# Two second-layer products at a time in chunks 3 to 6 of a memory-attention mixer

## The chip, the core and the metric

The kernel runs on one core of a Trainium2 chip. The time is the device time of one execution in microseconds (us). A run is repeated and the median taken; the kernel before took 741.93 us (three runs, 741.67 to 742.0). One execution was also recorded by the profiler, and the rows below come from it.

TensorE is written PE, its weight loads PEld, ScalarE is ACT, VectorE is DVE, GpSimd is POOL, SyncE (which issues most DMAs) is SP.

## The reference

Attention through 32 memory slots is followed by a mixer over tokens and one over channels:

```python
k_m = einsum('bhsm,bhsd->bhmd', softmax(phi), k)        # memory keys, v_m alike
attn = softmax(scale * q @ k_m.T) @ v_m                 # batch 8, heads 8, seq 576, head_dim 64
x = attn.transpose(0, 2, 1, 3).reshape(8, 576, 512)
h = relu(x.transpose(0, 2, 1) @ w_tok1) @ w_tok2        # 576 -> 256 -> 576
u = x + h.transpose(0, 2, 1)
out = u + relu(u @ w_ch1) @ w_ch2                       # 512 -> 1536 -> 512
```

All of it is float32. The kernel splits each operand into a high and a low part, and makes a product of three matmuls: high by high, high by low, low by high.

## The kernel before

The 8 x 576 rows are cut into nine chunks of 512 rows. Attention and the token mixer of a batch ("steps" of a quad of heads, functions whose names begin with step) are spread over the channel mixer of the chunks before it. Chunks 0 to 2 run the channel mixer plainly, chunks 7 and 8 together in another way at the end. The change touches chunks 3 to 6.

In these, the first layer (512 to 1536) is made in six pieces of 256 hidden features, numbered 0 to 5 here, by seven block products in the place of eight. The function `quarters` writes out one piece. The products are named by their operands, in the order "11", "21", "T2", "T1", "T3", "22", "T4". I call them A0, B1, A2, B3, A4, B5 and A6: the letter tells which PSUM tile takes the result (`qa` or `qb`), and the number the position. Each is six matmuls of 128x256 (line 335). A and B are the two buffers of one PSUM pool. A2 adds onto what A0 left in its bank, so it may start only when ACT has copied A0's result out (line 2167, `whole<-qa`). In the same way B3 follows the copy of B1, A4 that of A2, B5 that of B3 (`whole<-qb`), and A6 that of A4. The result of B5 is taken by DVE, that of A6 by ACT and DVE. A piece has five copies by line 2167, one each for A0 to A4. Each engine's instructions stand in its queue in the order in which the program writes them.

The second layer (1536 to 512) is accumulated in four banks, `acc0` to `acc3`, one for 128 output channels. For one hidden block of 128 features and one of the four channels it takes three matmuls of 128x512 (line 197). A piece brings two hidden blocks, so eight such groups of three stand in `todo`, and the next piece issues them between its products.

After each product comes `point(x)`, with x = 0, 0.5, ..., 3, and a last `point(3.5)` after `point(3)`. Each is a half slot. It first runs what the table `events` holds for it (`run`): loads, casts, a step of attention, the input preparation of a later chunk. Then `mix()` issues one group of three from `todo`. So a piece without steps reads on PE: A0, group, B1, group, A2, group, B3, group, A4, group, B5, group, A6, group, group.

Other work that the argument meets, all of it put between the products by `events`: the casts `a<-aT` (line 826, ACT) and their low halves (line 827, POOL) in `a_pair`; the casts `vv<-vh` (line 840, ACT) in `v_pairs`; the casts of the next chunk's operands `x<-u` and `xT<-t` (line 284, ACT); the exponential of the scores (line 776, ACT) after the subtraction of their maxima (line 771, DVE). `add` in `quarters` is line 2170 (DVE).

Of the kernel before, what the change touches and what calls it, by code (L numbers as in the profile page):

```python
# [27 lines left out]
def kernel(  # L28
# [30 lines left out]
    B, _, _, _, NC, _, D = kv.shape  # L59
# [78 lines left out]
    def relu_high(h, ps):  # L138
        nc.scalar.activation(out=h, in_=ps, func=AF.Relu)  # L139

    def relu_low(h, l, ps):
        nc.vector.scalar_tensor_tensor(  # L142
            out=l, in0=ps, scalar=0.0, in1=f32(h), op0=ALU.max, op1=ALU.subtract
        )
# [423 lines left out]
    def load_unit(n, eng=nc.scalar):  # L568
        m = n - 2 * NF * (DOUBLE - WIN + 1)
        if m >= 7 * NF // 4:  # L570
            return
        p, j = n // 4 % (NF // 2), n % 4
        t = sb.tile([P, 1024], F32R, tag="c1", name=f"unit{n}", bufs=NF)
        if m >= 0:
            units[n] = t.rearrange("p (o x m) -> p o x m", o=2, x=2)
            eng.dma_start(out=f32(t), in_=Sums2.to[:, m // (NF // 4), m % (NF // 4)])
            return
        units[n] = t.rearrange("p (o x a n) -> p o x a n", o=2, x=2, a=2)
        m = 512 if j == 3 else 1024
        nc.scalar.dma_start(out=f32(t)[:, :m], in_=sums[p].to[:, j, :m])  # L580
# [1416 lines left out]
    events = {}  # L1997
# [63 lines left out]
    for c in range(2, DOUBLE + 1):  # L2061
        h = 2 * NF * (c - 1)
# [18 lines left out]
    for c in range(DOUBLE):  # L2081
        h = 2 * NF * (c + 1)
# [15 lines left out]
    for p in range(NF // 2):  # L2098
        x, h = Sums2(p), 2 * NF * (WIN + min(p, 4)) + (8.5 if not p else (3.5, 1.5, 9.5)[max(p - 3, 0)])
# [8 lines left out]
    double, h = Double(DOUBLE), 2 * NF * DOUBLE  # L2108
# [14 lines left out]
    def run(h, *ks):  # L2123
        for k in ks:
            for fn, x in events.pop((h, k), ()):
                out = fn(*x)
                if callable(out):
                    out()
# [20 lines left out]
    def quarters(c, p):  # L2149
        ch, h, n = chunks[c], 2 * NF * c + 4 * p, 4 * ((c - WIN) * NF // 2 + p)  # L2150
        todo = [(x, f, a) for x, f in before if f < x.end for a in range(NKK)]
        before[:] = [(ch, 2 * p), (ch, 2 * p + 1)]
        (eh, el), (oh, ol) = ch.pieces(p)
        t0, t1 = slice(0, HW), slice(HW, CW)

        def mix(n=1):
            for x, f, a in todo[:n]:
                x.ch2(f, [a])
                if f == x.end - 1:
                    x.add(a)  # L2160
            del todo[:n]

        def tile(x):
            return pch.tile([P, CW], F32, tag="ch", name=f"{x}{p}" + ch.n, bufs=2)

        def out(to, ps):
            nc.scalar.copy(out=to, in_=ps[:, :HW])  # L2167

        def add(to, x, y):
            nc.vector.tensor_tensor(out=to, in0=x, in1=y, op=ALU.add)  # L2170

        def product(ps, k, name, first):
            if not k % 2:
                load_unit(n + k // 2 + AHEAD)
            ch.product(ps, units[n + k // 2][:, k % 2], name, first, name in ("21", "22", "T4"))

        if not whole:
            whole.append(sb.tile([P, 2, CW], F32, tag="c1", name="whole", bufs=NF))
        et, ot = whole[0][:, 0], whole[0][:, 1]

        def split_relu(h, l, x):
            relu_high(h, x)
            relu_low(h, l, x)

        def point(x):
            run(h + x, -1, 0, 1)
            mix()

        a = tile("qa")
        product(a, 0, "11", True)  # L2190
        out(et[:, t0], a)
        point(0)
        b = tile("qb")
        product(b, 1, "21", True)
        out(ot[:, t0], b)
        add(et[:, t0], et[:, t0], ot[:, t0])
        point(0.5)
        product(a, 2, "T2", False)
        out(et[:, t1], a)
        split_relu(eh[:, t0], el[:, t0], et[:, t0])  # L2200
        point(1)
        product(b, 3, "T1", True)
        out(ot[:, t0], b)
        point(1.5)
        product(a, 4, "T3", False)
        out(ot[:, t1], a)
        add(ot[:, t1], ot[:, t0], ot[:, t1])
        point(2)
        product(b, 5, "22", False)
        add(et[:, t1], b[:, :HW], et[:, t1])  # L2210
        split_relu(oh[:, t1], ol[:, t1], ot[:, t1])
        point(2.5)
        product(a, 6, "T4", False)
        split_relu(eh[:, t1], el[:, t1], et[:, t1])
        split_relu(oh[:, t0], ol[:, t0], a[:, :HW])
        point(3)
        point(3.5)

    for c in range(WIN, DOUBLE):
        for p in range(NF // 2):  # L2220
            quarters(c, p)
# [13 lines left out]
    for p in range(NF // 2):  # L2235
        h, n = 2 * NF * DOUBLE + 4 * p, n0 + 4 * p
# [63 lines left out]
    for i, name in enumerate(double.order[:-1]):  # L2300
        y = name in ("21", "T1", "22")
        for p in range(NF // 2):
            k = i * (NF // 2) + p
# [117 lines left out]
```

## Time and profile before

| | |
|---|---|
| median of three runs | 741.93 us (741.67 to 742.0) |
| the profiled execution | 741.64 us, of which the recorded span is 739.7 us |
| PE busy | 733.8 us, 99% of the span |
| PEld busy | 627.3 us, 85% |
| DVE, ACT, POOL busy | 494.2, 344.2, 72.1 us |
| products of chunks 3 to 6 (line 335) in the span | from 298.3 us to 614.7 us |

A row of the timeline gives the start in us from the beginning of the span, the duration, the engine, the line of the kernel, the operation, the output and inputs by name, partitions and elements, and a count if neighbouring instructions were merged. In brackets stands how long the engine sat idle before, and what released it. A matmul's duration covers its way through the array, so that neighbours overlap; the distance between starts is what a matmul costs. Weight loads run ahead of the matmul that uses them.

### The profile page before, as it was taken

Reading aid. Unit: us, or ns where it says so; the run is one execution under the profiler, and the core shown is the slowest. Engines: PE = TensorE matmul, PEld = TensorE weight load, DVE = VectorE, ACT = ScalarE, POOL = GpSimd, SP = SyncE. Lnnn points to the kernel's source line nnn. Section 1 sums busy time; section 2 is a strip of 40 time slices with the busy share of each in tenths; the row PEclk is TensorE's granted clock in tenths of the full one; section 3 lists DMA queues with packets and bytes.
Section 4 is the critical chain, followed back from the end, with each engine's and each line's share of the span. In section 5 each row is a group of like instructions: output and inputs, shape, how many; then the busy total and the mean of one; then the engine's idle time right before and its main releaser. Section 6 shows DMA issues by size and latency. Waiting matters only on the chain.

```text
span 739.7 us, 12859 instructions
## 1 busy us (share of the span) xinstructions
PE 733.8 (99%) x4889; PEld 627.3 (85%) x4889; DVE 494.2 (67%) x896; ACT 344.2 (47%) x742; POOL 72.1 (10%) x71
## 2 busy tenths in 40 slices
PE   9999999999999999999999999999999999999998
PEld 8678787787888888899898889888998998888887
DVE  4989873776567657766586738674676455655874
ACT  5789754242314243554463536363544462444431
POOL 1021014001022020110010101010101000000000
PEclk9999999999999999999999999999999999999999
DMA  9965530585825564869587858777667975776862
GB/s 358 415 230 178 218 106 1 136 260 145 260 90 169 168 201 107 285 189 310 163 270 252 252 214 228 259 212 278 167 203 246 305 218 174 256 256 208 272 217 86
DMA packets 98813, 158.33 MB, mean 214 GB/s; under 512 B 42208, under 2 KB 65632, under 8 KB 94304
## 3 DMA queue, kind: packets, MB, share of 16 engines
q1 hardware_dynamic: 80320, 98.92, 41.3%
q10 hardware_dynamic: 18432, 58.60, 25.0%
q8 instruction: 39, 0.64, 0.3%
q14 instruction: 22, 0.18, 0.1%
HBM read 121.57 MB, written 35.91 MB: 213 GB/s over the span
## 4 chain that ended last, share of the span: by engine, by line
PE 94%; DVE 3%; DMA 1%; ACT 1%; issue 0%; POOL 0%; POOLq 0%; DVEq 0%; ACTq 0%; SPq 0%
PE acc L197 29%; PE cp L174 12%; PE qa L335 9%; PE u L935 7%; PE qb L335 7%; PE e L455 7%; PE da L400 4%; PE db L400 3%; PE Ap L895 3%; PE Rp L914 1%; PE sp L754 1%; PE u L1617 1%; PE end L455 1%; PE sp L655 1%; PE u L1394 1%; PE pp L1269 1%
## 5 line engine op out<-in xcount | busy, mean ns | idle before, releaser
L197 PE MATMUL acc<-qhh,c 128*128 128x512 f32 x256 | 98.6, 395 | 0.0
L197 PE MATMUL acc<-hh,c 128*128 128x512 f32 x288 | 96.7, 395 | 0.0
L335 PEld LDWEIGHTS qb<-x,unit 128*128 128x128 f32 x432 | 60.9, 188 | 6.8 <-ACT whole L2167 0.7
L335 PEld LDWEIGHTS qa<-xT,unit 128*128 128x128 f32 x432 | 60.8, 188 | 6.8 <-ACT whole L2167 0.8
L197 PEld LDWEIGHTS acc<-hh,c 128*128 128x128 f32 x288 | 54.1, 188 | 14.5 <-issue 3.4
L335 PE MATMUL qa<-xT,unit 128*128 128x256 f32 x432 | 63.0, 281 | 0.0
L335 PE MATMUL qb<-x,unit 128*128 128x256 f32 x432 | 63.0, 281 | 0.0
L827 POOL TENSOR_TENSOR a<-aT,a 64x576 fp32r<-64x576 f32 x22 | 33.9, 1542 | 294.9 <-ACT a L826 294.1
L197 PE MATMUL acc<-hl,c 128*128 128x512 f32 x144 | 56.3, 391 | 0.0
L197 PEld LDWEIGHTS acc<-qhh,c 128*128 128x128 f32 x256 | 48.2, 188 | 9.5 <-issue 3.3
L197 PE MATMUL acc<-qal,c 128*128 128x512 f32 x192 | 53.7, 394 | 0.0
L142 DVE SCALAR_TENSOR_TENSOR hl<-cp,hh 128x512 fp32r<-128x512 f32 x36 | 24.7, 686 | 40.6 <-ACT hh L139 40.5
L174 PE MATMUL cp<-uh,c1h 128*128 128x512 f32 x144 | 51.3, 397 | 0.0
L197 PE MATMUL acc<-qhl,c 128*128 128x512 f32 x128 | 50.7, 396 | 0.0
L174 PE MATMUL cp<-ul,c1h 128*128 128x512 f32 x144 | 50.3, 390 | 0.0
L174 PE MATMUL cp<-uh,c1l 128*128 128x512 f32 x144 | 50.3, 390 | 0.0
L2170 DVE TENSOR_TENSOR whole<-whole 128x256 f32<-128x256 f32 x48 | 25.5, 531 | 37.0 <-ACT whole L2167 36.8
L2167 ACT COPY whole<-qa 128x256 f32<-128x256 f32 x72 | 26.8, 372 | 48.9 <-PE qa L335 47.0
L197 PEld LDWEIGHTS acc<-qal,c 128*128 128x128 f32 x192 | 32.7, 189 | 3.6
L142 DVE SCALAR_TENSOR_TENSOR qhl<-whole,qhh 128x256 fp32r<-128x256 f32 x48 | 22.1, 459 | 18.4 <-ACT qhh L139 18.1
L2167 ACT COPY whole<-qb 128x256 f32<-128x256 f32 x48 | 17.7, 369 | 34.9 <-PE qb L335 34.6
L174 PEld LDWEIGHTS cp<-uh,c1l 128*128 128x128 f32 x144 | 27.0, 188 | 5.7
(295 smaller groups left out, 1650.2 us busy)
## 6 DMA issues: line engine op xcount, KB each, us to landing
unit<-sums ACTq DMA_DIRECT2D x93, 512.0 KB, 4.3
kv<-in_kv_dram SPq DMA_DIRECT2D x12, 1280.0 KB, 8.8
rawc<-in_w_ch_dram SPq DMA_DIRECT2D x12, 1024.0 KB, 6.2
q<-in_q_dram SPq DMA_DIRECT2D x16, 576.0 KB, 6.2
unit<-sums SPq DMA_DIRECT2D x18, 512.0 KB, 4.8
unit<-sums ACTq DMA_DIRECT2D x30, 256.0 KB, 3.8
sums<-sums SPq DMA_DIRECT2D x12, 512.0 KB, 5.6
sums<-v SPq DMA_DIRECT2D x12, 512.0 KB, 6.9
```

What stands on the lines that cost most here:

```text
L142: nc.vector.scalar_tensor_tensor(out=l, in0=ps, scalar=0.0, in1=f32(h), op0=ALU.max, op1=ALU.subtract)
L174: nc.tensor.matmul(ps, l[:, a, w], r[:, a], start=n == 0, stop=n == len(mm) - 1)
L197: nc.tensor.matmul(ps, l_[f // 2][:, f % 2, a * P : (a + 1) * P], r[:, w], start=f == start and x == 0, stop=f == end - 1 and x == 2,)
L335: nc.tensor.matmul(ps[:, :HW], l, r, start=first and n == 0, stop=n == len(mm) - 1, skip_group_check=not first,)
L400: nc.tensor.matmul(ps, l, r, start=first and n == 0, stop=n == len(mm) - 1, skip_group_check=not first,)
L455: nc.tensor.matmul(ps, weights[:, x, m], r[:, w], start=first and n == 0, stop=last and n == 2, skip_group_check=name in ("T2", "T3", "22"),)
L655: nc.tensor.matmul(s.kvp[32 * i : 32 * i + 32, :KV], s.pt[:, i, j, :], s.kv[:, 4 * j + i], start=j == 0, stop=j == NC - 1,)
L827: s.low_eng.tensor_tensor(out=l, in0=s.aT[own], in1=f32(h), op=ALU.subtract)
L895: nc.tensor.matmul(ps[:, :TT], a, w, start=x == 0, stop=x == len(mm) - 1)
L935: nc.tensor.matmul(ps[:, :HALF], a, r, start=x == 0, stop=x == len(mm) - 1)
L2167: nc.scalar.copy(out=to, in_=ps[:, :HW])
L2170: nc.vector.tensor_tensor(out=to, in0=x, in1=y, op=ALU.add)
```

## The change

`point` no longer issues a group at every half slot. It counts the groups that are owed. If neither this half slot nor the next one holds a function whose name begins with `step`, the first owed group is held back and the two are issued together at the next point. Where a step is near, and at the end of a piece, everything owed is issued at once.

```diff
+        owed = [0]
...
         def point(x):
+            busy = any(k[0] in (h + x, h + x + 0.5) and fn.__name__.startswith("step")
+                       for k, v in events.items() for fn, _ in v)
             run(h + x, -1, 0, 1)
-            mix()
+            owed[0] += 1
+            if busy or owed[0] > 1 or x == 3.5:
+                mix(owed[0])
+                owed[0] = 0
```

The number of instructions is the same on every engine. ACT, POOL and SP issue theirs in the same order as before. On DVE one addition out of an `acc` bank in chunk 3 changes places with an `add` of the piece. PE's order changes in 17 of the 24 pieces; in the other seven (piece 3 of each chunk, and piece 0 of chunks 4 to 6) it is the same. A product into B now directly follows a product into A at 41 places more than before.

The first place is piece 5 of chunk 3, from A2 or B3 to B5. PE before, from B3 on; `qb` and `qa` are the PSUM tiles of the products, `acc` the banks of the second layer:

```order
L335 MATMUL qb_3_3901<-x_2649,unit_3809 128x256 x6
L197 MATMUL acc_3_3320<-qal_3_3705,c_1065 128x512
L197 MATMUL acc_3_3320<-qal_3_3706,c_1065 128x512
L197 MATMUL acc_3_3320<-qal_3_3705,c_1065 128x512
L335 MATMUL qa_3_3875<-xT_3_3028,unit_3844 128x256 x6
L197 MATMUL acc_3_3256<-qhh_3_3707,c_1065 128x512
L197 MATMUL acc_3_3256<-qhl_3_3708,c_1065 128x512
L197 MATMUL acc_3_3256<-qhh_3_3707,c_1065 128x512
L335 MATMUL qb_3_3901<-x_3_3080,unit_3844 128x256 x6
```

PE now at the same place, from A2 to B5:

```order
L335 MATMUL qa_3_3875<-xT_3_2986,unit_3806 128x256 x6
L335 MATMUL qb_3_3898<-x_2649,unit_3806 128x256 x6
L197 MATMUL acc_3_3299<-qal_3_3705,c_1065 128x512
L197 MATMUL acc_3_3299<-qal_3_3706,c_1065 128x512
L197 MATMUL acc_3_3299<-qal_3_3705,c_1065 128x512
L197 MATMUL acc_3_3320<-qal_3_3705,c_1065 128x512
L197 MATMUL acc_3_3320<-qal_3_3706,c_1065 128x512
L197 MATMUL acc_3_3320<-qal_3_3705,c_1065 128x512
L335 MATMUL qa_3_3875<-xT_3_3028,unit_3841 128x256 x6
L335 MATMUL qb_3_3898<-x_3_3076,unit_3841 128x256 x6
```

B3 has moved ahead of a group, to stand right behind A2; A4 has as many groups ahead of it as before; and the group between A4 and B5 has moved behind B5.

The second place is piece 1 of chunk 4, which begins with steps. PE before, from A2 to B5's neighbourhood:

```order
L335 MATMUL qa_4_4187<-xT_4_3949,unit_4110 128x256 x6
L197 MATMUL acc_4_4295<-qhh_4_4017,c_521 128x512
L197 MATMUL acc_4_4295<-qhl_4_4018,c_521 128x512
L197 MATMUL acc_4_4295<-qhh_4_4017,c_521 128x512
L335 MATMUL qb_4_4254<-x_3452,unit_4110 128x256 x6
L197 MATMUL acc_4_4307<-qhh_4_4017,c_521 128x512
L197 MATMUL acc_4_4307<-qhl_4_4018,c_521 128x512
L197 MATMUL acc_4_4307<-qhh_4_4017,c_521 128x512
L335 MATMUL qa_4_4187<-xT_4_3934,unit_4148 128x256 x6
```

PE now, from A2 on:

```order
L335 MATMUL qa_4_4187<-xT_4_3946,unit_4110 128x256 x6
L335 MATMUL qb_4_4254<-x_3452,unit_4110 128x256 x6
L197 MATMUL acc_4_4303<-qhh_4_4017,c_521 128x512
L197 MATMUL acc_4_4303<-qhl_4_4018,c_521 128x512
L197 MATMUL acc_4_4303<-qhh_4_4017,c_521 128x512
L197 MATMUL acc_4_4307<-qhh_4_4017,c_521 128x512
L197 MATMUL acc_4_4307<-qhl_4_4018,c_521 128x512
L197 MATMUL acc_4_4307<-qhh_4_4017,c_521 128x512
L335 MATMUL qa_4_4187<-xT_4_3934,unit_4148 128x256 x6
L335 MATMUL qb_4_4254<-x_4_4006,unit_4148 128x256 x6
```

The steps and the products up to A2 stand where they stood; from there on B3 and B5 each come one group earlier, and A4 where it was.

## Rows read from the trace of the kernel before

**Rows 1.** The page: its first line, and the shares of the chain of work that ended last, by engine.

```profile
span 739.7 us, 12859 instructions
...
PE 94%; DVE 3%; DMA 1%; ACT 1%; issue 0%; POOL 0%; POOLq 0%; DVEq 0%; ACTq 0%; SPq 0%
```

**Rows 2.** The waits of PEld between 300 and 628 us: who waited for whom, us in total, times, longest.

```profile
PEld qb L335 <- ACT whole L2167: 0.7, 2, 0.3
```

**Rows 3.** The timeline of PE in piece 5 of chunk 3: A0, a group, B1, the next group, and B5.

```profile
366.00 0.88 PE L335 MATMUL qa<-x,unit 128*128 128x256 f32 x6
366.72 0.86 PE L197 MATMUL acc<-qal,c 128*128 128x512 f32 x3
367.41 0.87 PE L335 MATMUL qb<-x,unit 128*128 128x256 f32 x6
368.12 0.86 PE L197 MATMUL acc<-qal,c 128*128 128x512 f32 x3
...
373.04 0.87 PE L335 MATMUL qb<-x,unit 128*128 128x256 f32 x6
```

**Rows 4.** The timeline of ACT, POOL and DVE in piece 5 of chunk 3: the copy of A0, a cast for POOL, POOL's two instructions, the first `add` of the piece on DVE, two casts of line 840, the copy of B3, and the second `add`.

```profile
366.97 0.37 ACT L2167 COPY whole<-qa 128x256 f32<-128x256 f32 x1 [1.53 <-PE qa L335]
...
367.24 0.67 ACT L826 CAST a<-aT 64x576 fp32r<-64x576 f32 x1
...
368.06 3.00 POOL L827 TENSOR_TENSOR a<-aT,a 64x576 fp32r<-64x576 f32 x2 [29.44 <-ACT a L826]
...
368.78 0.98 DVE L2170 TENSOR_TENSOR whole<-whole 128x256 f32<-128x256 f32 x1 [0.75 <-ACT whole L2167]
...
371.09 0.61 ACT L840 CAST vv<-vh 64x128 fp32r<-64x128 f32 x2 [0.49 <-POOL a L827]
...
372.25 0.37 ACT L2167 COPY whole<-qb 128x256 f32<-128x256 f32 x1
...
374.19 0.43 DVE L2170 TENSOR_TENSOR whole<-whole 128x256 f32<-128x256 f32 x1 [0.93 <-ACT whole L2167]
```

**Rows 5.** PE at 390 us, where two groups of the second layer stand side by side.

```profile
390.19 1.55 PE L197 MATMUL acc<-qal,c 128*128 128x512 f32 x6
391.57 0.64 PE L335 MATMUL qa<-x,unit 128*128 128x256 f32 x4
```

**Rows 6.** The timeline of PE in piece 0 of chunk 3: a product into A that directly follows one into B, and what follows it.

```profile
307.69 0.88 PE L335 MATMUL qa<-xT,unit 128*128 128x256 f32 x6
308.41 0.29 PE L935 MATMUL u<-a,vv 128*128 128x288 f32 x1
```

**Rows 7.** DVE and PE at the end of piece 1 and the beginning of piece 2 of chunk 4: the instruction that empties the bank of A6, and B1, which takes that bank next.

```profile
406.83 0.41 DVE L142 SCALAR_TENSOR_TENSOR qhl<-qa,qhh 128x256 fp32r<-128x256 f32 x1
...
407.71 0.87 PE L335 MATMUL qb<-x,unit 128*128 128x256 f32 x6
```

**Rows 8.** The copy of B3 and B5 in other pieces, two rows for each: piece 2 of chunk 3, piece 2 of chunk 5, piece 5 of chunk 5.

```profile
331.93 0.37 ACT L2167 COPY whole<-qb 128x256 f32<-128x256 f32 x1
332.72 0.87 PE L335 MATMUL qb<-x,unit 128*128 128x256 f32 x6
...
493.88 0.37 ACT L2167 COPY whole<-qb 128x256 f32<-128x256 f32 x1
494.29 0.98 PE L335 MATMUL qb<-x,unit 128*128 128x256 f32 x6
...
534.05 0.37 ACT L2167 COPY whole<-qb 128x256 f32<-128x256 f32 x1
534.85 0.40 PE L335 MATMUL qb<-x,unit 128*128 128x256 f32 x2
```

**Rows 9.** All engines in piece 2 of chunk 4: the copy of B3, the weight load of B5, B5 itself, the group behind it, and A0 of the next piece.

```profile
412.97 0.36 ACT L2167 COPY whole<-qb 128x256 f32<-128x256 f32 x1
...
413.38 0.76 PEld L335 LDWEIGHTS qb<-x,unit 128*128 128x128 f32 x6 [0.32 <-ACT whole L2167]
413.39 0.97 PE L335 MATMUL qb<-x,unit 128*128 128x256 f32 x6
...
414.19 0.40 PE L197 MATMUL acc<-qhh,c 128*128 128x512 f32 x1
...
417.14 0.64 PE L335 MATMUL qa<-x,unit 128*128 128x256 f32 x4
```

**Rows 10.** All engines in piece 1 of chunk 4: the copy of A2, the exponential, the copy of B3, and B5.

```profile
399.49 0.37 ACT L2167 COPY whole<-qa 128x256 f32<-128x256 f32 x1 [1.00 <-PE qa L335]
...
401.34 0.69 ACT L776 ACTIVATE S<-S 128x576 f32<-128x576 f32 x1 [1.16 <-DVE S L771]
...
401.93 0.35 ACT L2167 COPY whole<-qb 128x256 f32<-128x256 f32 x1
...
402.80 0.40 PE L335 MATMUL qb<-x,unit 128*128 128x256 f32 x2
```

**Rows 11.** The copy of B3 and B5 in pieces 1 and 2 of chunk 6.

```profile
563.09 0.35 ACT L2167 COPY whole<-qb 128x256 f32<-128x256 f32 x1
563.97 0.87 PE L335 MATMUL qb<-x,unit 128*128 128x256 f32 x6
...
573.55 0.37 ACT L2167 COPY whole<-qb 128x256 f32<-128x256 f32 x1
...
574.51 0.76 PE L335 MATMUL qb<-x,unit 128*128 128x256 f32 x5
```

## The prediction

> **What bounds the kernel now.** I read the page first. PE is busy for 99% of a span of 739.7 us, and the chain that ended last is PE's for 94% [rows 1]. So nothing can be won or lost but on PE itself: a matmul that costs more or less by what stands beside it, or a wait. The waits of PEld come next. Through chunks 3 to 6, B products waited for ACT's copies twice, for 0.7 us together [rows 2]. PE hardly waits there, and a change of its order can do two things only: alter the cost of neighbours, or bring a product to its bank before the copy has emptied it.
>
> For the second I read the timeline of a piece on PE, then on ACT. The reader is to see the margin between the end of a copy and the start of the product that reuses the bank. In piece 5 of chunk 3 B5 starts at 373.04 us [rows 3], and the copy of B3 ended at 372.25 + 0.37 = 372.62 [rows 4], 0.42 earlier. One product takes 368.12 - 367.41 = 0.71 us and one group 367.41 - 366.72 = 0.69 us [rows 3]. A margin of 0.42 is less than one group, and the change takes one group away from ahead of B5.
>
> **Neighbours.** 41 times two products now stand together, and 41 times two groups. Two groups side by side take 391.57 - 390.19 = 1.38 us [rows 5], against 2 x 0.69 to 0.70 apart: 0.00 to 0.02 us saved. A product directly behind another takes 308.41 - 307.69 = 0.72 us [rows 6], against 0.71: 0.01 lost. I take the sum as nothing, between a gain of 41 x 0.01 = 0.4 and a loss of 41 x 0.01 = 0.4 us. No other work hides it, as PE is the bound; it is the two sides that cancel.
>
> **What moves.** In a piece without steps the starts of the A products stay, and B1, B3 and B5 each start one group, 0.70 us, earlier. No instruction moves on ACT, POOL or SP, so no DMA is moved past anything, and unit loads are issued at their old places in ACT's queue. The one exchange on DVE, in chunk 3, stands in a piece whose additions out of `acc` feed no matmul of the piece; I cost it at nothing. The weight units are first read by A products, which do not move. The second-layer groups that are held back come later than before, so their operands are the readier. What is left are the banks. B3 waits for the copy of B1, which ACT takes soon after B1 and which moves with it. B1 takes the bank that A6 of the piece before had; the tightest such margin in a piece that changes is 407.71 - (406.83 + 0.41) = 0.47 us, in piece 2 of chunk 4 [rows 7]. It loses 0.70 and, as the sum below has it, wins back the 0.33 by which PE is late there: 0.10 is left, and I cost it at nothing (at worst 0.1 us in each of three such pieces). B5 is the one that matters.
>
> **Why B3's copy does not move with B3.** If ACT took the copy as soon as B3 ended, it would come 0.70 us earlier with it, and the margin would stay. In piece 5 of chunk 3 it doesn't. ACT's queue holds ahead of it two casts of line 840 and one of line 284. The first of them waited for POOL until 371.09, with ACT idle for 0.49 us [rows 4]. POOL's two instructions run from 368.06 for 3.00 us, and were released by a cast that follows the copy of A0; that copy was released by A0 [rows 4]. So the chain runs A0, copy, cast, POOL, casts, copy of B3. It begins with A0, which does not move, and contains neither B1 nor B3 as the last to arrive. The copy stays at 372.6 us.
>
> **First kind: pieces 2 and 5 of chunk 3, piece 5 of chunks 4 and 5.** The first of these four has 332.72 - (331.93 + 0.37) = 0.42 us of margin, the last 534.85 - (534.05 + 0.37) = 0.43 [rows 8]. B5 wants to start 0.70 earlier, and can start about 0.06 behind the end of the copy: in piece 2 of chunk 4, where B5 waits already, the copy ends at 412.97 + 0.36 = 413.33 and B5 starts at 413.39 [rows 9]. That is 0.70 - 0.42 + 0.06 = 0.34 us. A product that starts after such a wait also takes longer: 414.19 - 413.39 = 0.80 us to the next group, not 0.71, 0.09 more [rows 9]. Together 0.43 a piece, 4 x 0.43 = 1.7 us. Each counts anew, because the chain of the next one begins with its own A0, which comes as late as PE does.
>
> **Second kind: piece 1 of chunks 4, 5 and 6, piece 4 of chunks 4 and 5.** Here the copy of B3 stands behind the exponential of the scores, which follows DVE's subtraction, which follows the copy of A2 and its split [rows 10]. ACT sat idle for 1.16 us before it, so the chain again begins with an A product that stays. Margin in the first of these five 402.80 - (401.93 + 0.35) = 0.52 us [rows 10], in the last, piece 1 of chunk 6, 563.97 - (563.09 + 0.35) = 0.53 [rows 11]. Cost 0.70 - 0.52 + 0.06 + 0.09 = 0.33 each, 5 x 0.33 = 1.65 us.
>
> **Third kind: piece 2 of chunks 4 and 5.** B5 waits already [rows 8, 9], and cannot start before 413.39, however early PE comes. Behind it stood a group, A6 and two groups, until 417.14 [rows 9]. Now two groups, A6 and two groups follow: 0.80 + 1.38 + 0.71 + 1.38 = 4.27, until 417.66, which is 0.52 late. This chain hangs on DVE's work since the steps of piece 1, so the 0.33 us that piece 1 loses are within the 0.52 and not beside it. 2 x (0.52 - 0.33) = 0.4 us.
>
> **Piece 2 of chunk 6** has 574.51 - (573.55 + 0.37) = 0.59 us [rows 11], and PE comes 0.33 late from piece 1: 0.59 - 0.70 + 0.33 = 0.22, enough; nothing, at most 0.1. In piece 4 of chunk 3 the A products come earlier and the B products stay, so its chain comes earlier too: nothing. Pieces 4 and 5 of chunk 6 have fewer casts before the copy: nothing.
>
> **The sum.** 1.7 + 1.65 + 0.4 = 3.75 us. The profiled execution took 741.64 us, 1.9 us of it outside the span, which the change leaves alone: 741.6 + 3.75 = 745.4. The median of the runs is 0.3 above the profiled one: 741.93 + 3.75 = 745.7 us. From both sides: with all margins lost, the nine pieces of the first two kinds would cost 0.70 + 0.09 each and the two of the third 0.4 in all, 7.5 us; with no wait at all, and the neighbours' gain, it is 0.4 us less than before.
>
> **Rival: VectorE gets ahead of POOL.** Slower by more. In piece 5 of chunk 3 the copy of B1 now follows the first cast, which ends at 367.24 + 0.67 = 367.91 [rows 4], and ends near 368.25, so the first `add` (two operands from SBUF) is ready at about 368.3, where it came at 368.78. It took 0.98 us while POOL worked, and 0.43 us later in the piece [rows 4]: it was held until POOL's first instruction let go. POOL started at 368.06 [rows 4]. If the `add` came first by a little, POOL, and all that hangs on it, would start up to 0.43 later, in the four pieces of the first kind and the two of the third: 6 x 0.43 = 2.6 us more, 748.3. Against it stands 0.2 us by which POOL is still first. The Trainium skill (SBUF — State Buffer, "SBUF: two separate sides") says that a VectorE instruction with two SBUF inputs and a GpSimd instruction that reads SBUF share a port pair, and that whichever starts first holds it to its end. The 0.98 us agree with that; no run here shows POOL held by VectorE.
>
> **Rival: not slower.** If B3's copy were released by B3 in effect, because ACT's chain shortens as much as PE's (the copy of B1 and the second cast of line 826 do come 0.5 us earlier), B5 keeps its margin, the two waits of today go, and the neighbours give up to 0.4 us: 741.5 to 741.9. For it: 13 of the 24 pieces have such margins today that only 2 wait. Against it: the second cast is not what POOL's second instruction waits for, since the first one holds POOL until about 369.5; and ACT's idle time ends with POOL and DVE, not with PE [rows 4, 9, 10].
>
> **Rival: only the tightest pieces pay.** If the copies gain some 0.3 us, the first two kinds keep just enough margin, and what remains are the third kind's 2 x 0.52 and a few tenths: about 1.3 us, 743.2. The same if the 0.09 of a restart is not paid by a short wait and the wait shrinks by half.
>
> **How the numbers follow.** The forecast has 0.73, VectorE first 0.09, the tightest alone 0.08, not slower 0.10. A measurement of this kernel tells about 0.2%, 1.5 us, from no change. Forecast and VectorE first are slower by more: 0.82, and half of the tightest alone, 0.04, with the upper part of the last case 0.01: 0.87. Of the last case 0.03 is a gain that shows. The rest, 0.10, is the same. The likeliest's own range is 744.6 to 746.6. For 8 in 10 I go from 743.2, which takes in the tightest alone, to 747.4, short of VectorE first in all six pieces.
>
> **What will show it.** PEld's waits of B products for line 2167 rise from 2 to about 11 times, and from 0.7 to some 6 us (each contains about 0.27 us by which the load runs ahead). B5 takes 0.80 us where it waits. The copy of B3 in piece 5 of chunk 3 still starts 372.25 - 366.00 = 6.25 us behind A0. Products side by side take 0.72 us each and double groups 1.38. I am wrong if B3's copy follows B3 at 0.1 us, if POOL's first instruction starts later behind A0, or if waits appear in front of A products.

## The result and the profile after

The changed kernel took 746.18 us (median of six runs, 744.1 to 748.23), the kernel before 741.61 us beside it (six runs, 740.68 to 742.0). The ratio is 1.0062, 95% interval 1.0049 to 1.0075: 4.6 us slower, between 3.6 and 5.6. The profiled execution took 746.6 us.

The page of the changed kernel, its first line and the chain by engine, which answer to [rows 1]:

```profile
span 744.7 us, 12861 instructions
...
PE 86%; DVE 4%; ACT 3%; DMA 3%; POOL 2%; issue 1%; SPq 1%; ACTq 0%; POOLq 0%; DVEq 0%
```

PE had 94% of the chain in the kernel before. The 8% that it lost went to ACT, DVE, POOL and DMAs. A wait in front of PE shows here in this way: the chain leaves PE and walks back over the engines that made it wait. The shares move between executions too: run e7 below, the changed kernel again, has PE at 88%, and run e8, the kernel before again, at 91%.

The waits of PEld between 300 and 632 us, where [rows 2] had 0.7 us, 2 times:

```profile
PEld qb L335 <- ACT whole L2167: 3.6, 11, 0.4
```

The same for PE itself:

```profile
PE qa L335 <- DMA unit<-sums: 1.4, 1, 1.4
PE qb L335 <- ACT whole L2167: 0.4, 2, 0.2
```

B products wait for copies 11 times. The 1.4 on PE is the late arrival of a weight unit, and nothing of the kind stood in the trace before. It comes up again below.

The place on which the prediction rested, piece 5 of chunk 3 [rows 3, 4], in the timeline of the changed kernel:

```profile
367.49 0.88 PE L335 MATMUL qa<-x,unit 128*128 128x256 f32 x6
...
368.20 0.88 PE L335 MATMUL qb<-x,unit 128*128 128x256 f32 x6
...
368.92 1.55 PE L197 MATMUL acc<-qal,c 128*128 128x512 f32 x6
...
369.54 2.99 POOL L827 TENSOR_TENSOR a<-aT,a 64x576 fp32r<-64x576 f32 x2 [31.05 <-ACT a L826]
...
369.69 1.55 DVE L2170 TENSOR_TENSOR whole<-whole 128x256 f32<-128x256 f32 x1 [0.87 <-ACT whole L2167]
...
370.08 0.89 PEld L335 LDWEIGHTS qa<-xT,unit 128*128 128x128 f32 x6
370.31 0.88 PE L335 MATMUL qa<-xT,unit 128*128 128x256 f32 x6
...
370.90 0.79 PEld L335 LDWEIGHTS qb<-x,unit 128*128 128x128 f32 x6
371.02 0.88 PE L335 MATMUL qb<-x,unit 128*128 128x256 f32 x6
...
372.56 0.61 ACT L840 CAST vv<-vh 64x128 fp32r<-64x128 f32 x2 [0.47 <-POOL a L827]
...
373.13 0.87 PE L335 MATMUL qa<-xT,unit 128*128 128x256 f32 x6
...
373.72 0.37 ACT L2167 COPY whole<-qb 128x256 f32<-128x256 f32 x1
...
374.14 0.77 PEld L335 LDWEIGHTS qb<-x,unit 128*128 128x128 f32 x6 [0.35 <-ACT whole L2167]
374.14 0.98 PE L335 MATMUL qb<-x,unit 128*128 128x256 f32 x6
...
374.96 0.39 PE L197 MATMUL acc<-qhh,c 128*128 128x512 f32 x1
```

Read it from A0 at 367.49. B3 now starts 371.02 - 367.49 = 3.53 us behind it, but its copy starts 373.72 - 367.49 = 6.23 behind it, where it was 6.25 before [rows 3, 4]. So B5, which would follow A4 at 373.13 + 0.71 = 373.84, starts at 374.14, 0.05 us behind the end of the copy, and takes 374.96 - 374.14 = 0.82 us to the next group.

The second kind, piece 1 of chunk 4 [rows 10], and behind it the beginning of piece 2 [rows 7, 9]:

```profile
403.24 0.69 ACT L776 ACTIVATE S<-S 128x576 f32<-128x576 f32 x1 [1.16 <-DVE S L771]
...
403.83 0.35 ACT L2167 COPY whole<-qb 128x256 f32<-128x256 f32 x1
...
404.24 0.98 PE L335 MATMUL qb<-x,unit 128*128 128x256 f32 x6
...
408.74 0.42 DVE L142 SCALAR_TENSOR_TENSOR qhl<-qa,qhh 128x256 fp32r<-128x256 f32 x1
...
409.21 0.78 PEld L335 LDWEIGHTS qb<-x,unit 128*128 128x128 f32 x6
409.26 0.94 PE L335 MATMUL qb<-x,unit 128*128 128x256 f32 x6
```

ACT's idle 1.16 us in front of the exponential is the one of before to the hundredth, so the copy hangs on the same chain. And B1 at 409.26 has 409.26 - 409.16 = 0.10 us left behind the bank's release, the margin that the prediction gave it. It is not quite enough: the first weight load of B1 starts at 409.21, only 0.05 us ahead of its matmul, and the six matmuls of B1 take 0.94 us, where those of piece 5 of chunk 3 take 0.88.

The length of a piece is the distance from its A0 to the next A0. How much longer the pieces are than in the profiled execution of before, in us, for the changed kernel, a second execution of it (run e7 below) and four experiments:

| pieces | forecast | changed | again | e2 | e1 | e3 | e6 |
|---|---|---|---|---|---|---|---|
| first kind, each of 4 | 0.43 | 0.41 to 0.43 | 0.41 to 0.43 | 0.40 to 0.43 | 0.01 | 0.02 | 0.02 |
| second kind, each of 5 | 0.33 | 0.34 | 0.34 | 0.31 to 0.33, once 0.73 | 0.01, once 0.12 | 0.01 | 0.34, once 0.46 |
| third kind, each of 2 | 0.19 | 0.21, 0.22 | 0.22, 0.21 | 0.23 | 0.11, 0.10 | -0.17, -0.18 | -0.22, -0.23 |
| piece 2 of chunk 6 | 0 to 0.1 | 0.07 | 0.06 | 0.01 | 0.40 | 0.13 | 0.08 |
| piece 3 of chunk 3 | 0 | 1.58 | -0.03 | -0.03 | 1.57 | 1.62 | -0.01 |

From A0 of piece 0 of chunk 3 to the end of the 24 pieces the changed kernel took 323.33 us, 5.36 more than before. The kinds give 1.67 + 1.70 + 0.43, piece 2 of chunk 6 0.07, piece 3 of chunk 3 1.58, and the others -0.09 together.

One count in the text on the change above is loose: of the 41 new joins, 38 are a product into B behind one into A, and 3, in piece 4 of chunk 3, a product into A behind one into B.

### The profile page after: what moved, and what is told of

It reads as the page before. It is cut to its first block, busy times and chain, and to the rows that moved or that the text cites. A ratio compares the mean times of both kernels' runs of the same rounds, so it can differ in the third digit from the quotient of the medians.

```text
span 744.7 us, 12861 instructions
## 1 busy us (share of the span) xinstructions
PE 736.3 (99%) x4889; PEld 628.4 (84%) x4889; DVE 495.5 (67%) x896; ACT 345.1 (46%) x742; POOL 71.6 (10%) x71
## 4 chain that ended last, share of the span: by engine, by line
PE 86%; DVE 4%; ACT 3%; DMA 3%; POOL 2%; issue 1%; SPq 1%; ACTq 0%; POOLq 0%; DVEq 0%
PE acc L197 26%; PE cp L174 12%; PE qa L335 7%; PE u L935 7%; PE e L455 7%; PE qb L335 5%; PE da L400 4%; PE db L400 3%; PE Ap L895 3%; POOL a L827 2%; PE Rp L914 1%; PE u L1617 1%; DMA unit<-sums 1%; PE end L455 1%; PE sp L754 1%
## 5 line engine op out<-in xcount | busy, mean ns | idle before, releaser
L197 PE MATMUL acc<-qhh,c 128*128 128x512 f32 x256 | 94.7, 395 | 0.0
L335 PEld LDWEIGHTS qb<-x,unit 128*128 128x128 f32 x432 | 58.6, 189 | 6.5 <-ACT whole L2167 3.6
L2170 DVE TENSOR_TENSOR whole<-whole 128x256 f32<-128x256 f32 x48 | 28.2, 587 | 39.0 <-ACT whole L2167 39.0
L197 PE MATMUL acc<-qal,c 128*128 128x512 f32 x192 | 51.1, 393 | 0.0
```

Source lines behind the costliest of these rows:

```text
L197: nc.tensor.matmul(ps, l_[f // 2][:, f % 2, a * P : (a + 1) * P], r[:, w], start=f == start and x == 0, stop=f == end - 1 and x == 2,)
L335: nc.tensor.matmul(ps[:, :HW], l, r, start=first and n == 0, stop=n == len(mm) - 1, skip_group_check=not first,)
```

## The experiments

**Undoing B5's early place alone (e1).** B5 gets its group back, the joins ahead of it stay. (25 joins are left, not the 23 of the text below, which makes its rival 2.8 us.)

```diff
-            if busy or owed[0] > 1 or x == 3.5:
+            if busy or owed[0] > 1 or x >= 2:
```

> From half slot 2 on, every group is issued at its own point again, so that B5 has one group ahead of it as before the change; the joins ahead of it (A0 with B1, A2 with B3) stay. Theory (B5 comes to its bank before ACT has copied B3 out): the waits of B products for the copy by line 2167 fall from 11 back to 2, the profiled pieces of the first and second kind lose their 0.42 and 0.34 us, and the time is that of the kernel before within 0.5 us, some 3.8 us under the changed kernel. Rival (products and groups standing side by side cost by themselves): 23 of 41 joins are left, so about 4.6 x 23/41 = 2.6 us of the loss stays, 744.2 us.

Measured: 742.95 us (12 runs) against 742.27 of before (29 runs), ratio 1.0006 (0.9994 to 1.0017). The eleven waits are gone, the two of before among them, and with them the loss. In piece 5 of chunk 3 the copy of B3 starts 374.02 - 367.78 = 6.24 us behind A0, as ever, but B5 at 374.83 is behind it:

```profile
367.78 0.88 PE L335 MATMUL qa<-x,unit 128*128 128x256 f32 x6
...
374.02 0.37 ACT L2167 COPY whole<-qb 128x256 f32<-128x256 f32 x1
```

Another wait came up, in the view of PEld's waits:

```profile
PEld qb L335 <- DVE qhl L142: 1.0, 3, 0.3
```

The timeline of piece 2 of chunk 6, with A0, the instruction that empties A6's bank, and B1:

```profile
569.64 0.87 PE L335 MATMUL qa<-x,unit 128*128 128x256 f32 x6
...
570.16 0.42 DVE L142 SCALAR_TENSOR_TENSOR qhl<-qa,qhh 128x256 fp32r<-128x256 f32 x1
...
570.64 0.78 PEld L335 LDWEIGHTS qb<-x,unit 128*128 128x128 f32 x6 [0.33 <-DVE qhl L142]
570.64 0.98 PE L335 MATMUL qb<-x,unit 128*128 128x256 f32 x6
```

B1 would start at 569.64 + 0.71 = 570.35 and starts at 570.64. This is the margin of 0.47 less 0.70 of the prediction [rows 7], without the 0.33 by which piece 1 was late in the changed kernel. In the changed kernel the lateness of piece 1 pays for B1; with B5 back in its place B1 is the next to wait, which costs 0.40 us in piece 2 of chunk 6.

**B5's early place alone (e2).** Only the group ahead of B5 is held back, so B1 and B3 stand where they stood before.

```diff
-            if busy or owed[0] > 1 or x == 3.5:
+            if busy or owed[0] > 1 or x != 2:
```

> The other half: only the group between A4 and B5 is held back, and B1 and B3 stand where they stood before the change. Theory: B3's copy hangs on the ACT chain and not on B3, so B5 waits just as in the changed kernel: 0.42 us in each of four pieces, 0.34 in five, 0.2 more in two, 3.8 us over the kernel before. Rival (side by side costs by itself): 16 of 41 joins, 4.6 x 16/41 = 1.8 us over it. A second rival (B3 standing right behind A2 crowds ACT and makes the copy late): B3 is on its old place, so no more than the two old waits, 0 us.

Measured: 746.35 us (six runs), ratio 1.006 (1.0045 to 1.0075), the time of the whole change. The waits of PEld:

```profile
PEld qb L335 <- ACT whole L2167: 4.1, 12, 0.5
```

The timeline of piece 5 of chunk 3 from A0 on:

```profile
367.42 0.88 PE L335 MATMUL qa<-x,unit 128*128 128x256 f32 x6
...
371.64 0.87 PE L335 MATMUL qb<-x,unit 128*128 128x256 f32 x6
...
373.65 0.36 ACT L2167 COPY whole<-qb 128x256 f32<-128x256 f32 x1
...
374.07 0.97 PE L335 MATMUL qb<-x,unit 128*128 128x256 f32 x6 [0.15 <-ACT whole L2167]
```

B3 stands 371.64 - 367.42 = 4.22 us behind A0 here and 3.53 in the changed kernel, and its copy starts 6.23 behind A0 in both. So the copy takes no notice of where B3 stands, and moving B5 alone costs what the whole change costs. One piece more waits, piece 4 of chunk 3 (0.36 us), whose A products stay in this kernel.

**The copy of B3 moved up on ACT (e3).** The changed kernel, with the work of half slot 1 (the casts) behind the copy of B3 where no step stands there. The order on PE, DVE and POOL is the changed kernel's.

```diff
-        point(1)
+        if not quiet:
+            point(1)
         product(b, 3, "T1", True)
         out(ot[:, t0], b)
+        if quiet:
+            point(1)
```

Here `quiet` holds where nothing is owed and neither half slot 1 nor 1.5 has a step.

> The changed kernel with PE, DVE, POOL and SP in the same order; on ACT alone the copy of B3 stands ahead of what the half slot 1 puts into ACT's queue (the casts of lines 840 and 284, the exponential of line 776). Theory: B3's copy then starts about 0.1 us behind B3, B5 has over 1 us of margin in all pieces, its 11 waits go, also the two of the kernel before (0.6 us), and what is left of the change is the joins, 41 x 0.01 us or less: between 0.6 us under and 0.4 us over the kernel before. Rival (side by side costs by itself): as the changed kernel, 4.6 us over it. A third way: the casts come late by the copy's 0.4 us and something behind them waits instead; then a new wait shows in A6 or in a step.

Measured: 742.17 us (12 runs), ratio 1.0002 (0.9992 to 1.0013). The timeline of piece 5 of chunk 3:

```profile
371.00 0.88 PE L335 MATMUL qb<-x,unit 128*128 128x256 f32 x6
...
371.98 0.37 ACT L2167 COPY whole<-qb 128x256 f32<-128x256 f32 x1
...
372.56 0.61 ACT L840 CAST vv<-vh 64x128 fp32r<-64x128 f32 x2 [0.20 <-POOL a L827]
...
373.11 0.88 PE L335 MATMUL qa<-xT,unit 128*128 128x256 f32 x6
...
373.82 0.88 PE L335 MATMUL qb<-x,unit 128*128 128x256 f32 x6
```

The copy now starts 0.98 us behind the start of B3, before POOL is done, and B5 follows A4 at 373.82 - 373.11 = 0.71 without a wait. PE's order is the one that lost 4.6 us, and the loss is gone with ACT's order. It is the place of the copy in ACT's queue that makes B5 late. It also shows what the pairs are worth without the waits: nothing that these runs can tell from the kernel before.

**The same move on the kernel before (e4).**

```diff
-        point(1)
+        if quiet:
+            mix()
+        else:
+            point(1)
         product(b, 3, "T1", True)
         out(ot[:, t0], b)
+        if quiet:
+            run(h + 1, -1, 0, 1)
```

> The kernel before, with the same move on ACT: the copy of B3 ahead of what half slot 1 puts into ACT's queue; PE, DVE, POOL and SP in the order of the kernel before. Theory: the waits of B5 and A6 in piece 2 of chunks 4 and 5 go (0.3 us each in the trace), 0.6 us under the kernel before; together with the run on the changed kernel it gives what 41 joins cost without any wait. Rival (those waits are hidden or hang on something else): no change.

Measured: 741.78 us (11 runs), ratio 0.999 (0.9979 to 1.0001). The copy of B3 and B5 in piece 2 of chunk 4, where [rows 9] had a wait:

```profile
412.14 0.37 ACT L2167 COPY whole<-qb 128x256 f32<-128x256 f32 x1 [0.59 <-PE qb L335]
...
413.99 0.87 PE L335 MATMUL qb<-x,unit 128*128 128x256 f32 x6
```

The margin is 413.99 - 412.51 = 1.48 us; the pieces 2 of chunks 4 and 5 are 0.29 and 0.31 us shorter. This is the lowest median of the kernels measured beside these 29 runs of before, but 0.5 us cannot be told from before by these runs. Two waits for weight units, which the profiled execution of before lacks, stand against it in the one of e4: piece 0 of chunk 3 is 0.65 us longer and piece 3 is 0.91. Without these two pieces, those of e3 are together 0.5 us longer than those of e4, which has the same move on ACT and no new join. Of this, 0.38 is in piece 2 of chunks 4, 5 and 6, where B1 comes close behind the release of its bank. So some 0.5 us is what the 41 joins cost when B5 does not wait, B1's bank included.

**Weight units one pair of products earlier, on e4 (e5).** `AHEAD` is how many units a load stands ahead of the products that read it.

```diff
-    WIN, AHEAD = 3, 3
+    WIN, AHEAD = 3, 4
```

> The kernel before with the copy of B3 first (as in the run before it), and each weight unit loaded four units ahead in place of three (AHEAD = 4). It asks what the wait in piece 3 of chunk 3 is, which took 1.6 us in the changed kernel's profiled execution and none in that of the kernel before: A6 waited for its unit, 9.3 us on its way. Theory (the unit is late because its load is issued only 7 us ahead of A6, at a time when the DMA engines are near full): issued 2.8 us earlier, the wait goes in every execution, and the time is 0.5 to 1 us under the run with three ahead, some 741.0 us. Rival (the load is held by what ACT waits for ahead of it, or the DMA engines are full for longer): the wait stays and the time too.

Measured: 757.2 us (five runs) against 742.42 (nine runs), ratio 1.0201 (1.0176 to 1.0226). The expectation fell plainly: this kernel is about 2% slower. The waits of PEld:

```profile
PEld qa L335 <- ACT whole L2167: 15.0, 23, 1.9
```

The timeline at piece 2 of chunk 4, with A0, B1, the load of a unit on ACT's queue and the copy of A0:

```profile
409.57 0.88 PE L335 MATMUL qa<-x,unit 128*128 128x256 f32 x6
...
411.79 0.88 PE L335 MATMUL qb<-x,unit 128*128 128x256 f32 x6
...
412.71 0.33 ACTq L580 DMA_DIRECT2D unit<-sums  x1
413.07 0.37 ACT L2167 COPY whole<-qa 128x256 f32<-128x256 f32 x1 [3.12 <-PE qb L335]
```

The copy of A0 does not come until 413.07, 3.5 us after A0 started. ACT stood idle for 3.12 us in front of it, and what released ACT was a B product that started at 411.79. As the releaser and the code have it, the load of a unit needs the room of an older one, which that product still reads, and the copies stand behind the load in ACT's queue. Piece 3 of chunk 3 was 1.03 us longer than before, but not by the wait that this was to remove. That wait is one of A4 (the text above calls it A6), and in e5 no product of this piece waits for its unit; A2 and A4 wait for copies, like A4 here:

```profile
346.35 0.76 PEld L335 LDWEIGHTS qa<-xT,unit 128*128 128x128 f32 x6 [0.56 <-ACT whole L2167]
```

As the wait for the unit is also absent from some executions with three ahead (below), one profile of e5 does not show that the earlier load removed it.

**POOL out of the chain (e6).** The changed kernel, with the low halves of line 827 made by DVE from batch 4 on.

```diff
-            s.low_eng.tensor_tensor(out=l, in0=s.aT[own], in1=f32(h), op=ALU.subtract)
+            (nc.vector if s.b >= 4 else s.low_eng).tensor_tensor(out=l, in0=s.aT[own], in1=f32(h), op=ALU.subtract)
```

> The changed kernel, with the low halves of line 827 made by DVE in place of POOL from batch 4 on; PE's and ACT's order as in the changed kernel. Theory (in the first and third kind the copy of B3 hangs on POOL's 3.0 us through the casts of line 840; in the second on the exponential): the copy of B3 in pieces 2 and 5 comes 0.5 us earlier or more, the first kind's 0.42 us in four pieces and the third's 0.5 in two (0.2 more than piece 1's and the 0.3 of old waits) go, while the second kind's 0.34 in five pieces stay: 2.2 to 2.7 us under the changed kernel, 743.6 us. Rival (ACT's own load sets the copy, POOL beside it): no piece changes, 746.2 us. A worse way: DVE, with two more instructions, delays the additions out of the banks and other waits rise.

Measured: 753.79 us (five runs), ratio 1.0143 (1.0122 to 1.0164). The pieces answer the question, the total doesn't. Piece 5 of chunk 3:

```profile
377.36 0.88 PE L335 MATMUL qa<-x,unit 128*128 128x256 f32 x6
...
383.02 0.36 ACT L2167 COPY whole<-qb 128x256 f32<-128x256 f32 x1
...
383.72 0.88 PE L335 MATMUL qb<-x,unit 128*128 128x256 f32 x6
```

The copy comes 383.02 - 377.36 = 5.66 us behind A0 instead of 6.23, and B5 does not wait. The first kind loses 0.02 a piece, the third gains 0.22; the second, which has no POOL in its chain, stays at 0.34 to 0.46. But the kernel starts late. PE's waits in the first 60 us:

```profile
PE pp L1269 <- POOL mask L104: 12.5, 1, 12.5
```

POOL in the timeline of the start of the changed kernel:

```profile
1.22 0.29 POOL masks.py:199 TENSOR_SCALAR_AFFINE_SELECT ident<-ident 128x128 f32<-128x128 f32 x1 [0.29 <-POOL ident masks.py:197]
```

The same instruction in e6:

```profile
12.12 0.28 POOL masks.py:199 TENSOR_SCALAR_AFFINE_SELECT ident<-ident 128x128 f32<-128x128 f32 x1 [11.19 <-issue]
```

In the changed kernel PE waits 1.6 us there. These 10.9 us lie before any instruction that the edit touches, and POOL waits for nothing that the trace shows. Why is open; no run here tests it. The start, less the 2.9 us by which the 24 pieces are shorter than in the changed kernel, accounts for 8.0 of the 8.3 us by which the span is longer.

**Both kernels once more (e7, e8),** unchanged, one execution each, for the wait of piece 3 of chunk 3.

> The changed kernel once more, for another profile of piece 3 of chunk 3. If the wait of A6 for its unit belongs to the change, it is there again with 1.5 us; if it comes and goes with the DMA traffic of an execution, it may be anything from 0 to 2 us. The B products' waits should be the same to 0.05 us in every piece.

> The kernel before once more, with the same question: a wait in piece 3 of chunk 3 (none in its first profile) would show that it does not belong to the change.

Measured: the changed kernel 744.75 us, the kernel before 743.48. That wait is absent from this execution of the changed kernel (-0.03 us) and present in the one of before (1.66 us). Its form in the first execution of the changed kernel is a wait of A4 of piece 3, which the text above calls A6 (A6 starts 5 us later):

```profile
345.63 0.95 PE L335 MATMUL qa<-xT,unit 128*128 128x256 f32 x6 [1.38 <-DMA unit<-sums]
```

and in the kernel before, run again (ACT, then a matmul of the same piece):

```profile
337.16 0.62 ACT L135 CAST nat<-raw 128x512 fp32r<-128x512 f32 x1 [2.26 <-DMA raw<-rows]
...
337.83 0.39 PE L895 MATMUL Ap<-w1h,nat 128*128 128x256 f32 x1 [0.58 <-ACT nat L135]
```

Both begin with a DMA that lands late. The first form appeared in the changed kernel, in e3 and, with 0.7 us, in e4, whose order on PE is that of before; the second in e1 and in the kernel before. So it belongs to the execution, not to the change. Whether it comes more often with one order than with the other, these few profiles do not show. Without it the two executions of the changed kernel agree: 5.36 - 1.58 = 3.78 us over the 24 pieces in the first, and 321.71 - 317.97 = 3.74 in the second. The eleven waits read 3.6 us in both.

## Why the prediction was right

**The bound.** It held: the loss is waits of B5 in front of PE, and e3 takes it away by moving instructions on ACT alone.

**The copy that doesn't move with B3.** Shown: in piece 5 of chunk 3 it starts 6.25, 6.23, 6.24 and 6.23 us behind A0 in the kernel before, the changed one, e1 and e2, with B3 at two different places. That the low halves on POOL are part of that chain in the first kind, and not in the second, e6 shows: made by DVE, they let the copy start at 5.66.

**First kind.** 0.43 forecast, 0.41 to 0.43 measured. **Second kind.** 0.33 forecast, 0.34 measured. **Third kind.** 2 x 0.19 forecast, 0.43 together measured. The sum was 3.75, and the pieces named give 1.67 + 1.70 + 0.43 + 0.07 = 3.87. The restart, 0.80 us forecast for a B5 that has waited, is 0.82, and the start behind the copy 0.05 instead of 0.06.

**B1 and piece 2 of chunk 6.** The 0.10 left to B1 in piece 2 of chunk 4 stands in the trace as 0.10. That it was bought by the lateness of piece 1 was argued; e1 shows it, since B1 waits there. What the prediction put at nothing, at worst 0.1, is 0.06 for B1 (0.94 in place of 0.88) in piece 2 of chunks 4, 5 and 6 alike: the margin was counted to the matmul, and the weight load needs the bank too, as its wait in e1 shows. In piece 2 of chunk 6 it makes most of the 0.07 lost; in chunks 4 and 5 it is hidden in the wait of B5.

**Neighbours.** A pair of groups takes 1.39 us, and two products side by side 0.71 and 0.72. Three joins in a piece without waits cost 0.02 us (the first kind in e3), so a join costs some 0.007, less than the bound of 0.01. 41 of them would be at most 0.3 us lost, where I took nothing; the 0.5 us between e3 and e4 is more than that by B1's bank.

**The rivals.** VectorE ahead of POOL did not happen: POOL starts 369.54 - 367.49 = 2.05 us behind A0, where it was 2.06, and the `add` comes 0.15 behind it (forecast 0.2). It then takes 1.55 us in place of 0.98 and ends where it did, 371.24 - 367.49 = 3.75 us behind A0 (3.76 before). The Trainium skill (SBUF — State Buffer, "SBUF: two separate sides") has the engine that comes second blocked until the first one is done, and the longer 1.55 us agree with that. That POOL is held by VectorE no run here shows either. "Not slower" falls with the changed kernel and e2: the copies keep their time however early B3 comes. "Only the tightest pieces pay" falls with the table.

**What was off.** The total of PEld's waits was forecast at some 6 us and read 3.6, with 0.4 on PE. The step that failed is the 0.27 us by which I let every load run ahead. Behind a group the first load of a product starts 370.31 - 370.08 = 0.23 us before its matmul, but directly behind another product only 371.02 - 370.90 = 0.12, and B5 now stands there. In piece 5 of chunk 3 its load waits 0.35 us, and B5 itself is 374.14 - 373.84 = 0.30 late: 0.05 apart where the forecast had 0.27, and eleven times 0.22 are the 2.4 us that are missing. The count and the cost on PE were not touched by this. And among the signs that would prove me wrong I named waits in front of A products; one came, 1.4 us, but e7 and e8 show that it is not the change's. The measured difference of 4.6 us has an interval of 3.6 to 5.6; the piece lengths put the change at 3.7 to 3.9 of it, and the rest is not told from the spread of such waits. The six runs of before are also on the low side: the 29 that were made beside e1 to e4 have a median of 742.27, from which 746.18 is 3.9 away.

## What to carry to other kernels

Before an order is changed on the bounding engine, look for each buffer at what ends last in front of its release: a copy that stands in its queue behind work released by something else does not come earlier because its own producer does. Then the cost of moving the consumer up is the move less the margin, plus a small restart, and it can be read off the trace of before. The cure lies in the other queue (the copy ahead of the casts), but where PE is already busy for 99%, taking the waits away only gives back what the move cost.

## What the runs showed beside that

- A product that starts right after a wait for its bank takes 0.10 us more to the next instruction: 0.82 us, and 0.72 where a product stands directly behind another.
- Room can bind a load: with `AHEAD` at 4 one load held ACT for 3.12 us, and 23 waits of A products cost 15.0 us on PEld.
- With fewer instructions on POOL, one of its first came behind 11.19 us of idle time, where 0.29 us stood in the changed kernel (e6), without a releaser that the trace shows.
- The wait in piece 3 of chunk 3, about 1.6 us (0.9 in e4), comes and goes between executions of the same kernel.
